# A gated recurrence and a low-rank mixer with MLP: block-diagonal state on the full array, separate q and k banks, sliced weights, a new list schedule

## The chip, the cores and the metric

The kernel runs on one core of a Trainium2 chip. The metric is the device time of one execution in microseconds (us), the median of the runs shown.

## The reference

Four batches, eight heads, 768 steps, head size 48; all inputs float32. The first half is a gated linear recurrence ("GLA") per batch and head; its outputs, joined over the heads into x of 768 x 384, go through a mixer over the sequence of rank 32 and an MLP of width 1536.

```python
for t in range(S):
    state = alpha[:, :, t, :, None] * state + einsum('bhd,bhe->bhde', k[:, :, t], v[:, :, t])
    y[:, :, t] = einsum('bhd,bhde->bhe', q[:, :, t], state)
x = y.transpose(0, 2, 1, 3).reshape(B, S, H * D)
h = x.transpose(0, 2, 1) @ U @ V
u = x + h.transpose(0, 2, 1)
out = u + maximum(u @ w_ch1, 0.0) @ w_ch2
```

## The kernel before

**Tiling.** The sequence is cut into six chunks of 128 steps. For one chunk of one batch (`stage_gla`), all eight heads stand side by side in the free dimension (8 x 48 = 384 columns), and heads go to TensorE in four pairs; a head of a pair has 64 columns or partitions for its 48, the rest is zero. Four tiles (alpha, k, q, v; 192 KB each) are loaded by SyncE's queue (line 263). ScalarE takes the logarithm of alpha (line 265, tile `lt`), TensorE forms cumulative sums over the chunk with a triangular matrix (line 272) and the chunk's totals (line 274, four matmuls of one column), ScalarE makes `ai`, `aa` and `tot` by exponentials (lines 282 to 284). GpSimd scales k and q (lines 286 and 287, tiles `rk` and `rq`) and casts v (line 267, `rv`).

TensorE transposes `rk` and `rq` by pairs (line 295) into one PSUM bank; ScalarE copies the k half, VectorE the q half into `qk` (lines 304 and 306), both after both transposes. The scores (line 321, eight matmuls with 48 rows, at rows 0 or 64 of the array) go to a pair of banks, one for the even and one for the odd heads; VectorE multiplies each with the causal mask (line 332, `pm`). The output of the chunk, y, has eight matmuls of q with the state so far (line 347, 48 rows each, at rows 0 or 64) and eight of the masked scores with v (line 352, the full array, 48 columns), in two groups of four and four for each parity. ScalarE copies y into `xb` (line 363). The state of a head pair stands at partitions 0 to 47 and 64 to 111 with 48 columns: line 376 brings the old state into PSUM with an identity of 112 rows, line 381 adds k times v (eight matmuls of 48 columns, to partitions 0 or 64), and VectorE multiplies with `tot` (line 389, `st`).

After six chunks, `stage_mix` forms U times x (line 406, four at a time in columns 0, 32, 64 and 96 of the array), multiplies with V (line 417), adds x (VectorE, line 418, `ub`), and transposes the sum (line 427, copied by ScalarE, line 435, `uT`). `mlp1` has 24 products for a batch, each of three matmuls of 384 columns (line 447), with the ReLU on ScalarE (line 455) and VectorE (line 457) in turns; `mlp2` has six of twelve matmuls (line 471); VectorE adds u (line 478, `ou`), SyncE stores (line 479).

**PSUM.** Eight banks: two pairs for scores and y (`pair`), two banks (`gen`) for everything else of GLA and mix, two (`mlp`) for the MLP. In the last batch the MLP may use all.

**What sets the order.** Each step is an entry in a plan (class `Plan`) with an engine, a cost, what it reads and writes, and a priority. `Plan.run` simulates the engines with these costs, always takes the entry that can start first (by priority among those within 1 ns), and so gets one fixed list for each engine; the engines then run their lists in order, and wait where data come later than planned. GLA has priorities of 1000 and up, the MLP 5000 and up, so GLA goes first when both are ready. Weights are loaded by GpSimd's queue, U and V at the start, w1 and w2 after y of chunks 3 and 4 of batch 0 are copied (lines 250 and 253), each in one transfer with a cast to bfloat16. The plan gives these GpSimd entries a cost, but no time on the DMA engines; loads have 960 ns each.

Of the kernel before, what the change touches and what calls it, by code (L numbers as in the profile page):

```python
# [16 lines left out]

# [5 lines left out]
class Buf:  # L23


    def __init__(self, pool=None, slot=None):
        self.pools = pool if isinstance(pool, list) else ([pool] if pool else [])
        self.slot = slot
        self.home = None
        self.idx = 0  # L30
        self.left = 0
        self.last = 0.0
# [5 lines left out]
class Op:  # L38
    __slots__ = ("eng", "cost", "fn", "prio", "deps", "bufs", "n", "end", "users", "est", "i", "keep")


class Plan:


    LAT = {"PE": 230.0, "ACT": 120.0, "DVE": 120.0, "POOL": 150.0, "SP": 0.0, "DMA": 0.0}
# [6 lines left out]
    def add(self, eng, cost, fn, r=(), w=(), prio=0.0, keep=(), after=()):  # L52
        op = Op()
        op.eng, op.cost, op.fn, op.prio = eng, cost, fn, prio
        op.i = len(self.ops)
        op.deps, op.users, op.est, op.end = set(), [], 0.0, None
        op.keep = keep
# [17 lines left out]
        for k in list(r) + list(w) + list(keep):  # L75
# [9 lines left out]
    def run(self):  # L85
# [4 lines left out]
        ready = {}  # L90
        for op in self.ops:
            if op.n == 0:
                ready.setdefault(op.eng, []).append(op)
        clock = {}
        order = []
        dma = 0.0
        todo = len(self.ops)
        while todo:
            best = None
            for eng, cand in ready.items():  # L100
                now = clock.get(eng, 0.0)
                ok = []
                for op in cand:
                    t = op.est
                    for b in op.bufs:
                        if b.slot is None:
                            s = [x for p in b.pools for x in p.free if x is not None]
                            if not s:
                                t = None
                                break  # L110
                            t = max(t, min(s))
                    if t is not None:
                        ok.append((max(t, now), op))
                if not ok:
                    continue
                t0 = min(t for t, _ in ok)
                t1, op = min(((t, o) for t, o in ok if t <= t0 + 1.0), key=lambda x: (x[1].prio, x[1].i))
                if best is None or t1 < best[0]:
                    best = (t1, eng, op)
            if best is None:  # L120
                raise RuntimeError("the plan is stuck")
            t, eng, op = best
            for b in op.bufs:
                if b.slot is None:
                    _, n, x = min((f, n, x) for n, p in enumerate(b.pools) for x, f in enumerate(p.free) if f is not None)
                    p = b.pools[n]
                    p.free[x] = None
                    b.home, b.idx, b.slot = p, x, p.slots[x]
            ready[eng].remove(op)
            if eng == "SP":  # L130
                clock[eng] = t + 450.0
                dma = max(dma, t + 450.0) + op.cost
                op.end = dma + 1800.0
            else:
                clock[eng] = t + op.cost
                op.end = t + op.cost
            order.append((t, op))
            for b in op.bufs:
                b.left -= 1
                b.last = max(b.last, op.end + self.LAT[eng])  # L140
                if b.left == 0 and b.home is not None:
                    b.home.free[b.idx] = b.last
            for u in op.users:
                u.n -= 1
                lat = 0.0 if u.eng == eng and eng == "PE" else self.LAT[eng]
                u.est = max(u.est, op.end + lat)
                if u.n == 0:
                    ready.setdefault(u.eng, []).append(u)
# [3 lines left out]
        for _, op in order:  # L152
            op.fn()


def mm(*cols):
    return sum(max(c, 54) / 2.4 + 2.5 for c in cols)
# [3 lines left out]
def kernel(  # L161
# [22 lines left out]
    W = 112  # L184
    TW = S // 2

# [9 lines left out]

    ut_ones = const.tile([C, C], BF16, name="ut_ones")
# [5 lines left out]
    ones = const.tile([C, 1], BF16, name="ones")  # L203
    nc.vector.memset(ones, 1.0)

    w1_sb = const.tile([128, NCT, F], BF16, name="w1_sb")
    w2_sb = const.tile([128, NJ, DM], BF16, name="w2_sb")
    u_sb = const.tile([128, NC, R], BF16, name="u_sb")
    vm_sb = const.tile([128, S], BF16, name="vm_sb")

    io = Pool(slots("io", 40, [C, H, D], FP32))
# [11 lines left out]
    tots = Pool(slots("tot", 4, [128, HP, 1], FP32))  # L223
    qks = Pool(slots("qk", 3, [128, 8, C], BF16))
    pms = Pool(slots("pm", 3, [C, H, C], BF16))
    sts = Pool(slots("st", 4, [128, HP, D], BF16))
# [6 lines left out]
    s_zero = const.tile([128, HP, D], BF16, name="s_zero")  # L233
    nc.gpsimd.memset(s_zero, 0.0)
# [6 lines left out]
    def bf(bank):  # L241
        return bank.bitcast(BF16)

    def load_weights():
# [286 lines left out]
```

## Time and profile before

| what | value |
|---|---|
| median of the two runs shown | 211.76 us (211.25 and 212.28) |
| span of the profiled execution | 210.8 us; the median is 0.96 us above it |
| TensorE (PE) busy | 174.7 us, 83% |
| weight loads on PE | 107.5 us |
| VectorE, ScalarE, GpSimd busy | 97.4, 91.3, 60.8 us |
| moved by DMA | 26.48 MB, mean 126 GB/s |

The profiled execution's own time is its span; what lies around it isn't recorded. PE's time is of matmuls whose ends are modelled, so that followers overlap; the distance from one start to the next is what a matmul costs in a row. PEld is the load of the stationary operand, DVE VectorE, ACT ScalarE, POOL GpSimd, SP SyncE. A row's bracket gives the idle time before it on its engine and what ended it.

### The profile page before, as it was taken

The numbers are of one execution on the slowest core, as the hardware profiler recorded it, in microseconds if no ns is written. First come the engines' busy times: TensorE is split into PE (matmuls) and PEld (weight loads), VectorE is DVE, ScalarE is ACT, GpSimd is POOL, SyncE is SP. The second block draws the span as 40 slices with busy tenths as digits, with TensorE's granted clock in tenths as the row PEclk, the third lists the DMA queues.
The fourth block names the chain that finished last, engine by engine and source line by source line (L and its number), as shares of the span: only waits on it lengthen the run. The fifth ranks groups of instructions, "written<-read, shape, count | busy, mean of one in ns | idle before, by whom it ended". The sixth has DMA issues, their size and how long they took to land.

```text
span 210.8 us, 4417 instructions
## 1 busy us (share of the span) xinstructions
PE 174.7 (83%) x1732; PEld 107.5 (51%) x1732; DVE 97.4 (46%) x196; ACT 91.3 (43%) x209; POOL 60.8 (29%) x92
## 2 busy tenths in 40 slices
PE   1367868204899999899998499999999999999993
PEld 0245646001656655465665356565465656566561
DVE  1124526002657564766646557565542544433331
ACT  3255454003586654967465744643341450320100
POOL 8544663200074454435462830420000000000000
PEclk9999999999999999999999969999999999999999
DMA  7999999999999999999999950011102001212222
GB/s 127 179 188 190 165 190 178 189 190 173 192 168 197 164 195 156 198 174 196 171 212 159 222 164 2 3 37 37 40 0 99 13 3 37 75 40 75 75 74 77
DMA packets 106244, 26.48 MB, mean 126 GB/s; under 512 B 101104, under 2 KB 105840, under 8 KB 106224
## 3 DMA queue, kind: packets, MB, share of 16 engines
q1 hardware_dynamic: 103296, 23.60, 63.5%
q0 software_dynamic: 2928, 2.61, 7.8%
q8 instruction: 13, 0.21, 0.4%
q14 instruction: 7, 0.06, 0.1%
HBM read 24.08 MB, written 4.72 MB: 137 GB/s over the span
## 4 chain that ended last, share of the span: by engine, by line
PE 57%; DMA 16%; SPq 14%; ACT 3%; issue 3%; DVE 3%; POOL 1%; POOLq 0%; ACTq 0%
PE ps L471 21%; PE ps L447 20%; SPq L263 14%; DMA io<-in_alpha_dram 11%; DMA io<-in_v_dram 4%; PE ps L295 3%; PE ps L321 3%; PE ps L352 2%; PE ps L347 2%; DMA out_dram<-ou 2%; PE ps L427 2%; PE ps L417 2%; DVE ub L418 1%; PE ps L381 1%; PE ps L272 1%
## 5 line engine op out<-in xcount | busy, mean ns | idle before, releaser
L447 PE MATMUL ps<-uT,w_sb 128*128 128x384 bf16 x288 | 54.9, 329 | 0.5 <-ACT h1t L455 0.4
L471 PE MATMUL ps<-w_sb,h1t 128*128 128x384 bf16 x288 | 51.9, 326 | 0.0
L455 ACT ACTIVATE h1t<-ps 128x384 bf16<-128x384 f32 x48 | 23.4, 491 | 38.7 <-PE ps L447 38.6
L332 DVE TENSOR_TENSOR pm<-ps,maskc 128x512 bf16<-128x512 f32 x48 | 31.5, 685 | 18.8 <-PE ps L321 18.7
L471 PEld LDWEIGHTS <-h1t 128*128 128x128 bf16 x288 | 26.8, 97 | 16.4 <-issue 0.2
L447 PEld LDWEIGHTS <-w_sb 128*128 128x128 bf16 x288 | 26.2, 98 | 16.6 <-issue 2.2
L457 DVE TENSOR_SCALAR h1t<-ps 128x384 bf16<-128x384 f32 x48 | 26.2, 555 | 16.6 <-PE ps L447 16.0
L286 POOL TENSOR_TENSOR rk<-io,ai 128x384 bf16<-128x384 f32 x24 | 21.9, 913 | 37.6 <-ACT ai L282 35.2
L478 DVE TENSOR_TENSOR ou<-ub,ps 128x384 f32<-128x384 bf16 x24 | 13.3, 553 | 30.8 <-PE ps L471 27.8
L306 DVE COPY qk<-ps 128x512 bf16<-128x512 bf16 x24 | 10.1, 422 | 35.9 <-ACT utx L414 14.6
L265 ACT ACTIVATE lt<-io 128x384 bf16<-128x384 f32 x24 | 12.6, 524 | 32.5 <-DMA io<-in_alpha_dram 32.5
L267 POOL CAST rv<-io 128x384 bf16<-128x384 f32 x24 | 12.1, 503 | 38.6 <-DMA io<-in_v_dram 35.9
L287 POOL TENSOR_TENSOR rq<-io,aa 128x384 bf16<-128x384 f32 x24 | 21.9, 911 | 0.5 <-ACT tot L284 0.3
L304 ACT COPY qk<-ps 128x512 bf16<-128x512 bf16 x24 | 14.0, 583 | 13.0 <-PE ps L295 8.6
L321 PE MATMUL ps<-qk 48*128 48x128 bf16 x192 | 11.2, 247 | 5.3 <-ACT qk L304 3.4
L363 ACT CAST xb<-ps 128x384 bf16<-128x384 f32 x24 | 11.4, 477 | 9.4 <-PE ps L352 9.1
L352 PE MATMUL ps<-rv,pm 128*128 128x48 bf16 x192 | 13.8, 193 | 1.1 <-DVE pm L332 1.0
L282 ACT ACTIVATE ai<-ps 128x384 bf16<-128x384 f32 x24 | 11.9, 494 | 6.0 <-PE ps L274 5.0
L406 PE MATMUL ps<-xb,u_sb 128*32 128x384 bf16 x24 | 3.6, 376 | 12.8 <-ACT xb L363 11.6
L295 PEld LDWEIGHTS <-rq 128*128 128x128 bf16 x96 | 7.1, 108 | 13.6 <-issue 12.4
L418 DVE TENSOR_TENSOR ub<-xb,ps 128x384 bf16<-128x384 bf16 x24 | 12.4, 550 | 3.0 <-PE ps L417 2.6
L272 PE MATMUL ps<-lt,ut_ones 128*128 128x384 bf16 x24 | 9.1, 379 | 5.3 <-ACT lt L265 5.3
(44 smaller groups left out, 164.4 us busy)
## 6 DMA issues: line engine op xcount, KB each, us to landing
io<-in_alpha_dram SPq DMA_DIRECT2D x24, 192.0 KB, 4.5
io<-in_k_dram SPq DMA_DIRECT2D x24, 192.0 KB, 4.6
io<-in_q_dram SPq DMA_DIRECT2D x24, 192.0 KB, 4.4
io<-in_v_dram SPq DMA_DIRECT2D x24, 192.0 KB, 4.5
out_dram<-ou SPq DMA_DIRECT2D x24, 192.0 KB, 1.9
w_sb<-in_moe_w_ch_dram POOLq DMA_DIRECT2D x2, 1152.0 KB, 14.1
vm_sb<-in_moe_V_dram POOLq DMA_DIRECT2D x4, 48.0 KB, 5.2
u_sb<-in_moe_U_dram POOLq DMA_DIRECT2D x1, 48.0 KB, 5.4
```

Of the source, the lines that this page charges most:

```text
L263: P.add("SP", 960, lambda t=t, src=src: nc.sync.dma_start(t(), src[b, :, sl, :].rearrange("h t d -> t h d")), w=[t], prio=kk)
L286: P.add("POOL", 930, lambda: nc.gpsimd.tensor_tensor(rk()[:, :, 0:D], kt(), ai(), op=ALU.mult), r=[kt, ai], w=[rk], prio=pr + 2)
L287: P.add("POOL", 930, lambda: nc.gpsimd.tensor_tensor(rq()[:, :, 0:D], qt(), aa(), op=ALU.mult), r=[qt, aa], w=[rq], prio=pr + 2)
L304: nc.scalar.copy(qk()[:, o : o + HP, :], t[:, o : o + HP, :])
L321: nc.tensor.matmul(s2[:, par, p, :], lhsT=qk()[o : o + D, HP + p, :], rhs=qk()[o : o + D, p, :], start=(p == 0), stop=(p == HP - 1),)
L332: nc.vector.tensor_tensor(pm().rearrange("t (hp two) c -> t two hp c", two=2)[:, par], s2[:, par], maskc.to_broadcast([C, HP, C]), op=ALU. ...
L352: nc.tensor.matmul(y2[:, p, :], lhsT=pm()[:, 2 * p + par, :], rhs=rv()[:, 2 * p + par, :], start=(p == 0 and sprev is None), stop=(p == HP ...
L418: P.add("DVE", 550, lambda c=c, hb=hb: nc.vector.tensor_tensor(ub()[:, c, :], xb()[:, c, :], hb()[:, 0:DM], op=ALU.add), r=[hb, (xb, c)], ...
L447: nc.tensor.matmul(bank(hb)[:, 0:TW], lhsT=w1_sb[:, ct, jt * 128 : (jt + 1) * 128], rhs=uT()[:, ct, tt * TW : (tt + 1) * TW], start=(ct == ...
L455: P.add("ACT", 500, lambda jt=jt, hb=hb: nc.scalar.activation(h1()[:, jt, tt * TW : (tt + 1) * TW], bank(hb)[:, 0:TW], AF.Relu), r=[hb], w ...
L457: P.add("DVE", 560, lambda jt=jt, hb=hb: nc.vector.tensor_scalar_max(h1()[:, jt, tt * TW : (tt + 1) * TW], bank(hb)[:, 0:TW], 0.0), r=[hb] ...
L471: nc.tensor.matmul(bank(hb)[:, 0:DM], lhsT=h1()[:, jt, c * C : (c + 1) * C], rhs=w2_sb[:, jt, :], start=(jt == 0), stop=(jt == NJ - 1),)
```

## The change

**GLA.** The state of a head pair becomes a block-diagonal matrix of 128 x 96. To keep the other blocks zero, the chunk's totals get a second column for each pair, with -30000 added where row and column belong to different heads (`offd`, one more matmul of 8 columns with the identity), so that their exponential is zero. The state is then brought in with a full identity (one matmul of 384 columns) and k times v added by pairs (four matmuls of 96 columns on the full array); VectorE's multiplication has 128 x 384 elements. y has four matmuls of q with the state (128 rows, 96 columns) and eight with the scores; it is one group, in one bank. The zero state at the start of a batch is no longer added.

**Banks.** All eight banks form one pool. k and q are transposed into a bank each and copied to `kT` and `qT`, each as soon as its own transposes are done. An MLP product of batches 0 to 2 takes a bank only while more than four are free (`reserve`).

**Weights.** U and V are loaded as float32 by ScalarE's queue at the start and cast by GpSimd. w1 and w2 have three tiles each, loaded by GpSimd's queue in three transfers each, w1 when v of chunk 5 of batch 0 has landed, w2 when v of the first chunk of batch 1 has; a product waits only for the slice that it reads.

**Plan.** An entry may name several engines with a cost for each, and the engine that would finish it first takes it: the copies of `kT`, `qT`, `xb`, `utx`, `uT` and the ReLUs may go to ScalarE or VectorE. Weight transfers occupy the modelled DMA engines. A change of array mode costs 95 ns in the plan; steps of batches 1 to 3 get 150 ns of slack. Loads of all batches stand first in the list, and v of a chunk follows the next chunk's alpha. The MLP's priority puts it three chunks into the next batch (`LEAD`). In batch 0 VectorE scales q.

The core of the diff, with the plan's run shortened to what it models anew:

```diff
-    def add(self, eng, cost, fn, r=(), w=(), prio=0.0, keep=(), after=()):
+    def add(self, engs, fn, r=(), w=(), prio=0.0, mode="F", slack=0.0, after=()):
...
+                        s = sorted(x for x in b.pool.free if x is not None)
+                        if len(s) <= b.reserve:
+                            t = None
+                            break
+                        t = max(t, s[b.reserve])
...
+                key = (t1, t1 + op.engs[eng])
+                if best is None or key < best[0]:
+                    best = (key, eng, op)
...
-                clock[eng] = t + 450.0
-                dma = max(dma, t + 450.0) + op.cost
-                op.end = dma + 1800.0
+                dma = max(dma, t + 600.0) + cost
+                clock[eng] = max(t + 450.0, dma - 3500.0)
+                end = dma + 1600.0
+            elif op.mode == "DMA":
+                clock[eng] = t + 1000.0
+                dma = max(dma, t + 1000.0) + cost
+                end = max(t + 1000.0 + cost, t) + 2000.0
...
-    pair = Pool([ps[:, 0:2, :], ps[:, 2:4, :]])
-    gen = Pool([ps[:, 4, :], ps[:, 5, :]])
-    mlp = Pool([ps[:, 6, :], ps[:, 7, :]])
+    bank = Pool([ps[:, i, :] for i in range(8)])
...
+    nc.scalar.dma_start(u_in, moe_U.rearrange("(c p) r -> p c r", p=128))
+    for g in range(4):
+        nc.scalar.dma_start(v_in[32 * g : 32 * g + R, :], moe_V)
...
+    def f_w1(i):
+        nc.gpsimd.dma_start(w1_sb[i], moe_w_ch1.rearrange("(c p) f -> p c f", p=128)[:, :, i * FW : (i + 1) * FW])
...
+            for t, src, o in ((at, alpha, 0.0), (kt, k, 0.1), (qt, q, 0.2), (vt, v, 1.05)):
+                load(t, src, c, kk + o)
...
+            nc.tensor.matmul(cb()[:, DM : DM + 2 * HP], lhsT=ident, rhs=offd.rearrange("p a b -> p (a b)"), start=False, stop=False)
...
+        P.add({"DVE": 420} if b == 0 else {"POOL": 885}, lambda e: f_scale(e, rq, qt, aa), r=[qt, aa], w=[rq], prio=pr + 11, slack=sl)
...
+                if sprev is not None:
+                    nc.tensor.matmul(d2, lhsT=ident, rhs=sprev().rearrange("p a d -> p (a d)"), start=True, stop=False, skip_group_check=True)
+                for p in range(HP):
+                    nc.tensor.matmul(
+                        d2[:, p * 2 * D : (p + 1) * 2 * D],
+                        lhsT=rk()[:, 2 * p : 2 * p + 2, :].rearrange("t h w -> t (h w)"),
+                        rhs=rv()[:, 2 * p : 2 * p + 2, :].rearrange("t h d -> t (h d)"),
...
+                for p in range(HP):
+                    nc.tensor.matmul(y[:, 2 * p * D : (2 * p + 2) * D], lhsT=qT()[:, p, :], rhs=sprev()[:, p, :], start=(p == 0), stop=False)
...
+    def mlp_prio(b, x):
+        return ((b + 1) * NC + LEAD + x * NC) * 100.0
...
+            hb = Buf(bank, 0 if b == B - 1 else 4)
...
+            if b == 0 and c == NC - 1:
+                vt = tiles[b, c][3]
+                for i in range(3):
+                    P.add({"POOL": 2000}, lambda e, i=i: f_w1(i), r=[vt], w=[("w1", i)], prio=c * 100.0 + 30 + i, mode="DMA")
+                vt = tiles[1, 0][3]
+                for i in range(3):
+                    P.add({"POOL": 2400}, lambda e, i=i: f_w2(i), r=[vt], w=[("w2", i)], prio=-1, mode="DMA")
```

## Rows read from the trace of the kernel before

**Rows 1.** The page's slices: busy tenths, 40 slices of 5.27 us.

```profile
PE   1367868204899999899998499999999999999993
...
PEclk9999999999999999999999969999999999999999
DMA  7999999999999999999999950011102001212222
```

**Rows 2.** Windows: length, busy us (count) of each engine, clock, DMA share, GB/s.

```profile
37.00:51.00 14.00, 1.92 (x11) 0.89 (x11) 0.00 (x0) 1.22 (x3) 1.80 (x3) 1.00 1.12 182
57.00:126.00 69.00, 63.86 (x782) 39.53 (x782) 40.95 (x82) 44.63 (x110) 33.74 (x45) 0.98 1.11 184
126.00:207.40 81.40, 80.87 (x633) 48.11 (x627) 38.49 (x74) 25.68 (x53) 3.53 (x4) 1.00 0.12 42
207.40:210.80 3.40, 0.00 (x0) 0.00 (x0) 0.55 (x1) 0.00 (x0) 0.00 (x0) 1.00 0.18 63
124.00:125.00 1.00, 1.00 (x9) 0.83 (x8) 0.45 (x1) 0.13 (x1) 0.00 (x0) 0.50 0.02 8
```

**Rows 3.** Timeline, 29 to 58 us: start, length, engine, line, idle before.

```profile
29.73 0.83 POOL L250 DMA_DIRECT2D w_sb<-in_moe_w_ch_dram  x1
...
31.68 0.49 POOL L267 CAST rv<-io 128x384 bf16<-128x384 f32 x1
...
32.12 1.09 POOL L253 DMA_DIRECT2D w_sb<-in_moe_w_ch_dram  x1
...
36.70 0.34 PE L352 MATMUL ps<-rv,pm 128*128 128x48 bf16 x4
...
49.21 0.52 ACT L265 ACTIVATE lt<-io 128x384 bf16<-128x384 f32 x1 [12.32 <-DMA io<-in_alpha_dram]
49.64 0.46 ACT L363 CAST xb<-ps 128x384 bf16<-128x384 f32 x1
...
50.15 0.48 PE L406 MATMUL ps<-xb,u_sb 128*32 128x384 bf16 x1 [11.63 <-ACT xb L363]
...
57.06 0.65 PE L447 MATMUL ps<-uT,w_sb 128*128 128x384 bf16 x3
```

**Rows 4.** DMA queues, 29 to 50 us: packets, MB, share of 16 engines.

```profile
q0 software_dynamic: 1952, 2.36, 66.4%
q1 hardware_dynamic: 7383, 1.39, 48.0%
```

**Rows 5.** The weight tile's transfers, issue to landing.

```profile
DMA to landing us min/median/max: 11.2/14.1/16.9
```

**Rows 6.** Groups by line on PE: line 272, first 0 to 57, then 57 to 126 us.

```profile
L272 PE MATMUL ps<-lt,ut_ones 128*128 128x384 bf16 x8 | 3.8, 476 | 5.3 <-ACT lt L265 5.3
...
L272 PE MATMUL ps<-lt,ut_ones 128*128 128x384 bf16 x15 | 4.9, 330 | 0.0
```

**Rows 7.** Timeline of PE, 62 to 66 us.

```profile
62.14 0.25 PE L376 MATMUL ps<-st,ident 112*112 112x192 bf16 x1
...
62.53 0.66 PE L447 MATMUL ps<-uT,w_sb 128*128 128x384 bf16 x3
63.13 0.40 PE L321 MATMUL ps<-qk 48*128 48x128 bf16 x8
63.46 0.40 PE L295 MATMUL ps<-ident,rk 128*128 128x128 bf16 x4
...
63.91 0.33 PE L272 MATMUL ps<-lt,ut_ones 128*128 128x384 bf16 x1
...
64.18 1.14 PE L447 MATMUL ps<-uT,w_sb 128*128 128x384 bf16 x6
65.25 0.27 PE L347 MATMUL ps<-st,qk 48*128 48x48 bf16 x4
...
65.85 0.27 PE L352 MATMUL ps<-rv,pm 128*128 128x48 bf16 x4
65.97 0.65 PE L447 MATMUL ps<-uT,w_sb 128*128 128x384 bf16 x3
```

**Rows 8.** The page's groups: the causal mask.

```profile
L332 DVE TENSOR_TENSOR pm<-ps,maskc 128x512 bf16<-128x512 f32 x48 | 31.5, 685 | 18.8 <-PE ps L321 18.7
```

More of the change, by code (lines that the diff above doesn't have):

```diff
@@ L38 @@
 class Op:
[L39 removed]
+    __slots__ = ("engs", "fn", "prio", "deps", "bufs", "n", "users", "est", "i", "mode", "slack", "eng", "t")
 class Plan:
[L45 removed]
+    LAT = {"PE": 215.0, "ACT": 155.0, "DVE": 145.0, "POOL": 110.0, "SP": 0.0}
+    SWITCH = 95.0
     def __init__(self):
@@ L74, in add @@
         bufs = []
-        for k in list(r) + list(w) + list(keep):
+        for k in list(r) + list(w):
             b = k[0] if isinstance(k, tuple) else k
@@ L96, in run @@
         dma = 0.0
+        mode = "F"
         todo = len(self.ops)
         while todo:
-            best = None
[L100 to L115, printed above, removed]
+            per = {}
+            for op in ready:
+                t = op.est
+                for b in op.bufs:
+                    if b.slot is None:
+                        s = sorted(x for x in b.pool.free if x is not None)
[3 more added lines that the diff above has]
+                        t = max(t, s[b.reserve])
+                if t is None:
+                    continue
+                for eng in op.engs:
+                    per.setdefault(eng, []).append((max(t, clock.get(eng, 0.0)), op))
+            best = None
+            for eng, ok in per.items():
@@ L138, in run @@
+            order.append(op)
+            done = end + (0.0 if op.mode == "DMA" else self.LAT[eng])
             for b in op.bufs:
                 b.left -= 1
-                b.last = max(b.last, op.end + self.LAT[eng])
-                if b.left == 0 and b.home is not None:
-                    b.home.free[b.idx] = b.last
+                b.last = max(b.last, done)
+                if b.left == 0:
+                    b.pool.free[b.idx] = b.last
             for u in op.users:
                 u.n -= 1
-                lat = 0.0 if u.eng == eng and eng == "PE" else self.LAT[eng]
@@ new lines, with stage_loads, load @@
+    LEAD = 3.0
+    tiles = {}
+    def stage_loads(b):
+        def load(t, src, c, key):
+            sl = slice(c * C, (c + 1) * C)
+            P.add({"SP": 1030.0}, lambda e: nc.sync.dma_start(t(), src[b, :, sl, :].rearrange("h t d -> t h d")), w=[t], prio=key)
+        for c in range(NC):
+            at, qt, kt, vt = (Buf(io) for _ in range(4))
+            tiles[b, c] = at, qt, kt, vt
+            kk = b * NC + c
+            for t, src, o in ((at, alpha, 0.0), (kt, k, 0.1), (qt, q, 0.2), (vt, v, 1.05)):
+                load(t, src, c, kk + o)
@@ L330, in f_mask @@
         def f_mask(par):
[L331 to L351 removed]
+            s2 = sc[par]().rearrange("p (hp c) -> p hp c", c=C)
@@ L352, in f_y @@
+        yb = Buf(bank)
+        def f_y(e):
+            y = yb()[:, 0:DM]
+            if sprev is not None:
+                for p in range(HP):
+                    nc.tensor.matmul(y[:, 2 * p * D : (2 * p + 2) * D], lhsT=qT()[:, p, :], rhs=sprev()[:, p, :], start=(p == 0), stop=False)
+            for h in range(H):
                 nc.tensor.matmul(
-                    y2[:, p, :], lhsT=pm()[:, 2 * p + par, :], rhs=rv()[:, 2 * p + par, :],
-                    start=(p == 0 and sprev is None), stop=(p == HP - 1),
-                )
```

336 lines of the change are left out of this document (155 added, 181 removed).

## The prediction

> **What bounds the kernel now.** I read the page's slices first [rows 1]. A digit is 5.27 us. The DMA row is full up to 121 us, while the PE row has a weak start, two nearly empty slices from 37 to 47 us (2 and 0), and is full after 58 except for a 4 from 116 to 121. So neither resource bounds the whole: loads pace the first part, TensorE the last. The stretches [rows 2] make it exact. From 37 to 51 us PE is busy 1.92 of 14 us while DMA moves 182 GB/s; from 57 to 126 it is busy 63.86 of 69; from 126 to the last matmul at 207.4 it is busy 80.87 of 81.40; the tail, an addition and the last store, takes 3.4 us. After about 57 us the end is therefore PE's remaining work plus what PE loses in it.
>
> The hole is the second thing to understand, and the timeline shows it [rows 3]. GpSimd issues both weight transfers at 29.73 and 32.12 us. The last product of batch 0 (y of chunk 5) starts at 36.70, but its copy into xb runs on ScalarE at 49.64: ahead of it in ScalarE's queue stood a logarithm that waited 12.32 us for an alpha tile. PE then waited 11.63 us for that copy, and the first MLP product came at 57.06. The queues tell why the alpha was late [rows 4]: between 29 and 50 us the weights moved 2.36 MB and the loads 1.39 MB, that is 7 tiles in 21 us where 184 GB/s would bring 19. The weights landed 11.2 and 16.9 us after issue [rows 5].
>
> The clock has to be read with care. Its row says 1.00 from the start, yet the 384-column matmul of line 272 has a mean of 476 ns before 57 us and 330 ns from 57 to 126 [rows 6]. The 146 ns between them are nearly what 384 columns differ by at 1.2 and 2.4 GHz (160 ns), so I take the early part as half clock by duration, and all terms below from the later part. Once, after the slice in which PE was at four tenths [rows 1], the granted clock itself reads 0.50, its lower level [rows 2].
>
> **The old time as a sum.** MLP products follow each other at (1.14-0.33)/5 = 0.162 us [rows 7]; 576 of them (288 on each of lines 447 and 471) are 93.6 us. A GLA chunk on PE, from one start to the next with pipelined tails taken off, costs [rows 7]: cumulative sums 63.91 to 64.18, 0.27; transposes 63.46 to 63.91, 0.45; scores 63.02 (62.53 plus three products) to 63.46, 0.44; y 65.155 (64.18 plus six products) to 65.97, 0.815; state 62.14 to 62.53, 0.39. Together 2.365 us, and 17 chunks after 57.06 are 40.2. From 57.06 to 207.40 are 150.3 us, so 16.6 remain: the mixes of batches 1 to 3 and lost time. I carry these over unchanged as one term.
>
> **The change part by part.**
> *y.* Eight 48-row state products become four full-array products of 96 columns; eight score products stay. The last four score products before an MLP product take 65.85 to 65.97, 0.03 each; the four row-tiled ones take 65.25 to 65.45, 0.05 each with the change of array mode inside. New cost: low end four of 96 columns at the MLP's rate per column (0.042) and eight at 0.03, 0.41; high end twelve at 0.05, 0.60. No mode change is left inside, so I take 0.42: 0.395 us saved.
> *State.* One 384-column product (0.162) and four of 96 columns (0.042 to 0.056, the latter being a transpose, 0.45/8) give 0.33 to 0.39 for 0.39. I take 0.36.
> *Sums.* One more product of 8 columns: 0.03, bounded by the 0.027 that each of the four one-column products takes ((0.27-0.162)/4) and 0.05.
> Transposes and scores issue as many matmuls as before. Per chunk 2.365-0.395-0.03+0.03 = 1.97 us (1.93 to 2.2).
>
> Against the first step speaks a rule. The four row-tiled products took 0.20 us [rows 7], mode change included. The Trainium skill, "TensorEngine Tiling (Array Packing)", sections Tiling Modes and Performance Considerations, gives up to 2x for a contraction of 64 rows or fewer through two row tiles at once, and says too that a change of tiling mode drains the array. The trace cannot split the 0.20 us into the two; by the first sentence alone the untiled products would give the saving back and the sum would be 201, by the second the change removes the drains and it stays at the value below.
>
> *Other engines.* The masks keep 685 ns each [rows 8]. The new state multiplication covers 192 columns more on VectorE, at the masks' rate 0.26 us; VectorE was busy 40.95 of 69 us [rows 2] and doesn't bind, so I cost it at nothing: MLP products cover the longer chain, and uncovered it is 17 x 0.26, 4.4 us. Separate banks and copies for q and k, and the scaling of q on VectorE in batch 0, shorten a chain that the loads pace there and MLP products hide later: nothing gained in the sum. The five small loads on ScalarE's queue stand ahead of the first logarithm; in the first slice PE is at one tenth [rows 1] and chunk 0 waits for loads, so a delay of some 2 us is absorbed; uncovered it would cost those 2 us.
>
> *Weights.* They wait for v of chunk 5, and w2 for v of the next batch's first chunk. The old v of chunk 5 was cast at 31.68 [rows 3]; one load is now ahead of it, so w1 goes at about 32. By the old share [rows 4] half of the bytes takes some 10 us: thirds at about 36, 39 and 42. Loads meanwhile bring one tile in about 3 us, so v of chunk (1,0) lands at about 42, and w2 runs from 42 to 52. Behind the w2 issues on GpSimd stand, by their priority of -1, the scalings and the cast of chunks (1,0) and (1,1), and PE's transposes wait for those.
>
> *Start of the MLP.* Before, 7.42 us lay between the xb copy (49.64) and the first MLP product (57.06). If the copy follows its y, at 34 to 37.5, the MLP starts at 40 to 46; I take 43, and no slice of w1 is awaited then. But chunks (1,1) and (1,2) still load at a third of the rate until 52, and a list that expects them earlier makes an in-order engine wait, as the logarithm did. I charge 2 us (0 to 8).
>
> The sum: 43 + 2 + 93.6 + 17.5 chunks x 1.97 (34.5; half of a chunk more is left at 43 than at 57) + 16.6 + tail 3.4 = 193.1 us of span. The old span of 210.8 stands 0.96 below the median of 211.76; with the same margin the forecast is 194 us, of which 12 of the gain come from the hole and 7 from y, less what the earlier start still has to do.
>
> **The rivals.**
> *Hole kept (0.12).* The slices split a transfer, not its share of the DMA engines; an alpha may again hold ScalarE for 12 us. For it: 66.4% against 48.0% for the queues in that stretch [rows 4]. Against it: w2 comes later and MLP work is there to run. With the start at 53 in place of 45 the sum gives 202.
> *Loads bind between batches 0 and 1 (0.08).* 48 tiles of 0.197 MB, the weights and the first stores are some 13 MB; at 184 GB/s the next batch's last tile lands near 72, its MLP can start near 84 (some 5 us from v's cast to y, 31.68 to 36.70, and 7.4 on), and PE's work from 45 (23.4 of MLP, six chunks of 1.97, a mix of some 2.5) ends near 83. The two meet; a few stores more and PE idles up to 5 us: 199.
> *Tiling was worth its drains (0.05).* The four full products multiply half zeros; if they take as long as the eight that ran two at a time and the mode changes were cheap, the chunk stays at 2.365: 17.5 x 0.395 = 6.9 us more, 201. The matmul part then doesn't do what it says. For it: 0.05 a product is also what untiled products could take. Against it: 0.03 a product right before an MLP product, the same array mode [rows 7]. The rule above is this case.
> *Fewer losses (0.09).* The one pool of eight banks and the new latencies remove half of some 9 us (16.6 less three mixes of 2.5) and the 2 us charged: 187 or, with a start at 41, 185.
> *Slower (0.04).* An MLP product of batches 0 to 2 takes a bank only while more than four are free; before, two banks were its own. A chunk's two score banks alone are held for one and two masks (0.685, 1.37). If waiting chunks hold four banks most of the time, MLP work slides behind the last chunk: PE loses a quarter of the 85 us from 45 to 130, 21 us, and the time is 215. It decides from about 17 us of such idling on. Against it: a chunk comes every 6.3 us (37.7/6), and its masks hold the score banks for under a quarter of that.
>
> **How the numbers follow.** My forecast case (0.62) spans 189 to 200: start 40 to 46, charge 0 to 4, chunk up to 2.05. The range of 185 to 204 adds the faster case, the first three rivals, the charge of 8 and the 2.2 us chunk. About 2% is what a measurement here can tell from no change, so faster means under 207.5. All but the slower rival and the worst of the kept hole (a second stall of the same kind after it) are under that: faster 0.91, same 0.05, slower 0.04.
>
> **What the new profile would show.** The first product of line 447's successor at 40 to 46 us; y's group at about 0.42 us between its neighbours and a chunk near 1.97; PE busy over 90% from 52 on; three w1 landings before 44, and w2 after 50. It would be wrong if PE's first dense slice is again near 57, if four 96-column products take over 0.3 us, or if PE idles between 70 and 85.

## The result and the profile after

The changed kernel takes 187.78 us (186.91 and 188.65) against 211.76: ratio 0.885, 95% interval 0.876 to 0.894. Forecast were 194, 185 to 204. On another chip, beside the experiments, it took 186.48, ratio 0.8835 (0.878 to 0.889). Times are medians of all executions shown; the ratios leave out executions more than 1.5% slower than the fastest of the same kernel. The profiled execution is the one of 188.65, with a span of 186.9; its last matmul ends at 182.9.

The page's slices, now of 4.67 us, answer to [rows 1]:

```profile
PE   0157878788999999889999969999999999999991
```

The two empty slices near 40 us are gone. What is left in their place is an emptier first slice.

Three windows, to be read against [rows 2]: the hole, the stretch from 57 to 126 us, the stretch from there to the new last matmul; and a fourth at a drop of the clock (the clock is the share of TensorE's full clock that was granted, 0.50 its lower level):

```profile
37.00:51.00 14.00, 12.82 (x113) 8.01 (x113) 8.96 (x17) 8.99 (x21) 7.07 (x10) 1.00 1.25 190
57.00:126.00 69.00, 65.82 (x754) 44.15 (x752) 44.04 (x84) 42.30 (x103) 30.21 (x41) 0.98 0.90 188
126.00:182.90 56.90, 56.64 (x452) 34.67 (x446) 20.99 (x39) 26.61 (x57) 3.53 (x4) 1.00 0.13 45
112.00:118.00 6.00, 5.70 (x54) 4.45 (x54) 2.85 (x7) 4.82 (x14) 5.49 (x7) 0.72 1.05 219
```

From 37 to 51 us PE is busy 12.82 us, where it was 1.92. From 57 to 126 us PE is a little fuller than before (65.82 of 69 us against 63.86), and there is less for it to do.

The timeline where the hole was, for [rows 3]: the load of alpha of chunk (1,1), that is chunk 1 of batch 1, the transfers of w1, the last score products of y of chunk 5, its copy into xb, the transfers of w2, the logarithm of chunk (1,1) and the first MLP product:

```profile
27.98 0.99 SPq L286 DMA_DIRECT2D io<-in_alpha_dram  x1
...
32.49 2.47 POOL L275 DMA_DIRECT2D w_sb<-in_moe_w_ch_dram  x3
...
36.56 0.46 PE L409 MATMUL ps<-rv,pm 128*128 128x48 bf16 x7 [0.38 <-DVE pm L368]
...
37.06 0.48 ACT L257 CAST xb<-ps 128x384 bf16<-128x384 f32 x1 [0.36 <-PE ps L409]
37.20 2.29 POOL L278 DMA_DIRECT2D w_sb<-in_moe_w_ch_dram  x3
...
38.48 0.53 ACT L301 ACTIVATE lt<-io 128x384 bf16<-128x384 f32 x1
...
43.99 1.14 PE L472 MATMUL ps<-uT,w_sb 128*128 128x384 bf16 x6
```

That load of alpha, from issue to landing:

```profile
DMA to landing us min/median/max: 3.7/3.7/3.7
```

The end of y of chunk 5 is no earlier than before (its last group starts at 36.56 against 36.70). But its copy now stands ahead of the logarithm in ScalarE's list and runs at 37.06 in place of 49.64, and the first MLP product comes at 43.99 in place of 57.06. A second thing changed with it: the alpha that held up ScalarE before was then issued at 30.76, behind the first weight transfer at 29.73, and landed 18.4 us later; now it is issued at 27.98, ahead of the first weight transfer at 32.49, and lands 3.7 us later. Its logarithm would not have waited even ahead of the copy. So the new order of the loads and the new list both work against this hole, and no run separates the two.

The DMA queues from 29 to 50 us, for [rows 4], and the weights from issue to landing, for [rows 5]:

```profile
q0 software_dynamic: 2525, 2.17, 65.2%
q1 hardware_dynamic: 9408, 1.78, 51.8%
```

```profile
DMA to landing us min/median/max: 6.6/10.2/13.9
```

The weights again take the larger share, but the loads got 1.78 MB where it was 1.39.

PE at 45 to 59 us, for [rows 7]:

```profile
45.85 0.65 PE L472 MATMUL ps<-uT,w_sb 128*128 128x384 bf16 x3
46.43 0.40 PE L358 MATMUL ps<-qt,kt 48*128 48x128 bf16 x8
46.76 0.40 PE L337 MATMUL ps<-ident,rk 128*128 128x128 bf16 x4
46.99 0.33 PE L308 MATMUL ps<-lt,ut_ones 128*128 128x384 bf16 x1
...
47.29 0.38 PE L337 MATMUL ps<-ident,rq 128*128 128x128 bf16 x4
47.51 1.14 PE L472 MATMUL ps<-uT,w_sb 128*128 128x384 bf16 x6
...
49.10 2.12 PE L472 MATMUL ps<-uT,w_sb 128*128 128x384 bf16 x12
51.06 0.33 PE L407 MATMUL ps<-st,qt 128*128 128x96 bf16 x4
51.23 0.36 PE L409 MATMUL ps<-rv,pm 128*128 128x48 bf16 x8
51.44 0.32 PE L381 MATMUL ps<-st,ident 128*128 128x384 bf16 x1
...
51.77 6.99 PE L472 MATMUL ps<-uT,w_sb 128*128 128x384 bf16 x42
```

Read as before: scores 46.34 (45.85 plus three products) to 46.76, 0.42; transposes 0.23 and 0.22; sums 46.99 to 47.29, 0.30; y 51.06 to 51.44, 0.38, of which the four products of 96 columns take 0.17; state to 51.77, 0.33. A chunk costs 1.88 us.

### The profile page after: what moved, and what is told of

Same layout as the page of the kernel before. It is cut to its first block, busy times and chain, and to the rows that moved or that the text cites. A ratio compares the mean times of both kernels' runs of the same rounds, so it can differ in the third digit from the quotient of the medians.

```text
span 186.9 us, 4147 instructions
## 1 busy us (share of the span) xinstructions
PE 163.1 (87%) x1592; PEld 105.7 (57%) x1592; DVE 93.5 (50%) x185; ACT 98.8 (53%) x229; POOL 57.4 (31%) x86
## 4 chain that ended last, share of the span: by engine, by line
PE 72%; DVE 5%; DMA 3%; issue 1%; ACT 1%; DVEq 0%; ACTq 0%
PE ps L472 25%; PE ps L496 25%; PE ps L337 5%; PE ps L358 3%; DMA io<-in_alpha_dram 3%; PE ps L409 3%; DVE pm L368 2%; PE ps L450 2%; DVE ub L441 2%; PE ps L308 2%; PE ps L440 2%; PE ps L383 1%; PE ps L407 1%; PE ps L381 1%; PE ps L311 1%
## 5 line engine op out<-in xcount | busy, mean ns | idle before, releaser
L472 PE MATMUL ps<-uT,w_sb 128*128 128x384 bf16 x288 | 51.9, 326 | 0.0
L483 ACT ACTIVATE h1t<-ps 128x384 bf16<-128x384 f32 x78 | 37.8, 490 | 19.3 <-PE ps L472 19.2
L326 POOL TENSOR_TENSOR rq<-io,aa 128x384 bf16<-128x384 f32 x18 | 16.5, 915 | 2.1 <-PE ps L472 2.1
L393 DVE TENSOR_TENSOR st<-ps,tot 128x384 bf16<-128x384 f32 x20 | 11.1, 554 | 8.4 <-PE ps L383 8.4
L337 PE MATMUL ps<-ident,rk 128*128 128x128 bf16 x96 | 11.1, 249 | 2.8 <-POOL rk L326 2.8
L409 PE MATMUL ps<-rv,pm 128*128 128x48 bf16 x192 | 10.6, 192 | 2.5 <-DVE pm L368 2.5
L358 PE MATMUL ps<-qt,kt 48*128 48x128 bf16 x192 | 10.8, 240 | 2.2 <-DVE qt L259 2.1
L485 DVE TENSOR_SCALAR h1t<-ps 128x384 bf16<-128x384 f32 x18 | 9.6, 556 | 6.1 <-PE ps L472 5.8
L257 ACT COPY kt<-ps 128x512 bf16<-128x512 bf16 x14 | 8.2, 588 | 7.8 <-PE ps L337 7.7
L337 PE MATMUL ps<-ident,rq 128*128 128x128 bf16 x96 | 10.8, 244 | 1.7 <-DVE rq L326 1.6
## 6 DMA issues: line engine op xcount, KB each, us to landing
w_sb<-in_moe_w_ch_dram POOLq DMA_DIRECT2D x6, 384.0 KB, 10.2
```

Source lines behind the costliest of these rows:

```text
L257: nc.scalar.copy(dst, src)
L326: eng.tensor_tensor(dst()[:, :, 0:D], a(), x(), op=ALU.mult)
L337: nc.tensor.matmul(t[:, p, :], lhsT=ring()[:, 2 * p : 2 * p + 2, :].rearrange("t h w -> t (h w)"), rhs=ident, start=True, stop=True, is_tr ...
L358: nc.tensor.matmul(sc[par]()[:, p * C : (p + 1) * C], lhsT=kT()[o : o + D, p, :], rhs=qT()[o : o + D, p, :], start=(p == 0), stop=(p == HP ...
L409: nc.tensor.matmul(y[:, h * D : (h + 1) * D], lhsT=pm()[:, h // 2, h % 2, :], rhs=rv()[:, h, :], start=(h == 0 and sprev is None), stop=(h ...
L472: nc.tensor.matmul(hb()[:, 0:TW], lhsT=w1_sb[jt * 128 // FW][:, ct, jt * 128 % FW : jt * 128 % FW + 128], rhs=uT()[:, ct, tt * TW : (tt + ...
```

## The experiments

Each kernel was timed beside the kernel before on its chip. The changed kernel was run once more beside its first three variants and is the measure for all of them; for those on other chips the ratios are the better comparison. Except in this second run and in the one with sixteen matmuls, the plan is run anew with the edit, so that a list can differ in other places too.

> The changed kernel once more, beside the others: 187 to 189 us by every theory; its interval says what differences of the others can be read.

Measured: 186.48. Its profile bears out the reading of [rows 6]. In the profiles before and after, the clock row stays at 1.00 through the whole early part; in this one it recorded early changes (windows):

```profile
30.00:40.00 10.00, 8.09 (x69) 4.55 (x68) 5.70 (x11) 4.16 (x11) 7.92 (x11) 0.50 1.13 194
...
43.00:45.00 2.00, 2.00 (x21) 1.42 (x22) 0.98 (x2) 1.20 (x3) 0.60 (x2) 1.00 1.27 184
```

The clock is half from 30 to 40 us and full from 43 on, as the durations of this kernel say too (a sum of 384 columns takes 0.48 us at 30 us in the profile after, 0.33 at 46.99).

**Old y in the new kernel.**

```diff
-        yb = Buf(bank)
+        ys = Buf(bank), Buf(bank)
...
+                    nc.tensor.matmul(y[:, p, :], lhsT=qT()[o : o + D, p, :], rhs=sprev()[o : o + D, p, par * D : (par + 1) * D], start=(p == 0), stop=False)
```

> Only y goes back to two banks, row-tiled state products of 48 rows and 48 columns in groups of four, and two copies into xb; the block-diagonal state stays. If y's matmuls carry a term of the gain, each of the 15 chunks of batches 1 to 3 that have a state costs 0.38 to 0.82 us more or less as the rows before and after show, a difference of 0.435 us, so 6.5 us more than the changed kernel: about 194. If the list and the banks carry the gain and PE had slack, 188 to 190.

Measured: 190.19, ratio 0.8998 (0.896 to 0.9036), 3.7 us more. On PE the cost is back whole:

```profile
63.95 0.81 PE L503 MATMUL ps<-w_sb,h1t 128*128 128x384 bf16 x4
64.70 0.27 PE L408 MATMUL ps<-st,qt 48*128 48x48 bf16 x4
64.90 0.27 PE L410 MATMUL ps<-rv,pm 128*128 128x48 bf16 x4
65.10 0.27 PE L408 MATMUL ps<-st,qt 48*128 48x48 bf16 x4
65.30 0.27 PE L410 MATMUL ps<-rv,pm 128*128 128x48 bf16 x4
65.42 0.38 PE L337 MATMUL ps<-ident,rq 128*128 128x128 bf16 x4
```

From 64.60 (63.95 plus four products) to 65.42 y takes 0.82 us. The three groups of four with a change of mode behind them take 0.20 us each, the last one, with none behind it, 0.12. Only the 15 chunks that have a state have the row-tiled products. So 15 times 0.435, or 6.5 us of matmul time, cost 3.7, near what the second theory said: this kernel lost less elsewhere.

The scores are row-tiled too, but their list alternates between the two halves of the rows, where y's has four of one half in a row. The products that have started by a moment tell the two apart (windows of the scores' line in the profile after, whose first product starts at 46.43, then of y's state products here, first at 64.70):

```profile
46.40:46.45 0.05, 0.02 (x2) 0.02 (x4) 1.00 0.93 134
...
64.65:64.73 0.08, 0.03 (x1) 0.04 (x2) 1.00 0.05 19
```

Of the scores two have started within 0.02 us, one of each half; of y's products one alone within 0.03.

**Sixteen matmuls without a change of mode.**

```diff
-                for p in range(HP):
-                    nc.tensor.matmul(y[:, 2 * p * D : (2 * p + 2) * D], lhsT=qT()[:, p, :], rhs=sprev()[:, p, :], start=(p == 0), stop=False)
+                for h in range(H):
+                    nc.tensor.matmul(y[:, h * D : (h + 1) * D], lhsT=qT()[:, h // 2, :], rhs=sprev()[:, h // 2, h % 2 * D : (h % 2 + 1) * D], start=(h == 0), stop=False)
```

> y's four state products of 96 columns become eight of 48 columns on the full array, the list untouched: as many matmuls as before the change, but no change of array mode. If the mode changes were the cost, eight products take 0.03 us each, 0.24 instead of 0.17, and 15 chunks add 1 us: about 189. If the number of matmuls was the cost, most of 6.5 us comes back: 192 to 194.

Measured: 187.01, ratio 0.8846 (0.88 to 0.8892): no difference from the changed kernel.

```profile
51.36 0.36 PE L407 MATMUL ps<-st,qt 128*128 128x48 bf16 x8
51.56 0.36 PE L409 MATMUL ps<-rv,pm 128*128 128x48 bf16 x8
51.76 0.32 PE L381 MATMUL ps<-st,ident 128*128 128x384 bf16 x1
```

Sixteen matmuls take 0.40 us (51.36 to 51.76), 0.025 each. The same number with two row-tiled groups among them took 0.815, or 0.41 us more for four changes of mode, some 0.1 for a change; the groups of the run before, 0.20 with a change behind and 0.12 without, say nearly the same. The number of matmuls cost next to nothing: 0.40 for sixteen against 0.38 for twelve.

**Whole weights.**

```diff
-    FW = F // 3
-    JW = NJ // 3
+    FW = F
+    JW = NJ
...
     def f_w1(i):
+        if i == 0:
```

> Each weight in one transfer at the same place of the same list. If the gates and the order close the hole and the slices do nothing, all of w1 lands near 43 to 46 us, the first MLP product moves by under 2 us from 44.0 and the time by under 2 us: 187 to 190. If the slices matter, the first MLP product waits for the whole of w1 and the time rises by 3 us or more, to 191 or above.

Measured: 186.74, ratio 0.8824 (0.8772 to 0.8875). First MLP product at 43.94. The slices do nothing here: a whole weight lands 10.3 to 13.6 us after its issue, w1 thus by about the time when uT is ready.

**The matmuls alone, in the kernel before.** The block-diagonal state, y and sums of the change; old weights, banks and plan.

```diff
+            nc.tensor.matmul(cb()[:, DM : DM + 2 * HP], lhsT=ident, rhs=offd.rearrange("p a b -> p (a b)"), start=False, stop=False)
...
+        P.add("PE", 500, f_y, r=rs + [(pm, 0), (pm, 1)], w=[yb], prio=pr)
```

> The kernel before with the block-diagonal state, its four-matmul y and state and the eight-column mask alone; weights, banks and plan stay as they were. If the matmuls are a term of their own, 17 chunks after the hole lose 0.485 us each (2.365 against 1.88 read off the traces): 8 us less, 203, with the first MLP product still near 57 us. If the saving turns into waits, because the hole and the loads set the pace, 207 to 211.

Measured: 206.49, ratio 0.9784 (0.972 to 0.9847): 4.3 us less, about half of what the matmuls save and a little under the second theory's range. First MLP product at 56.15. The clock took part of the gain: it was at its lower level here when the MLP began, from 56.15 to some 60 us, where the kernel before had three products in 0.65 us at 57.06 and so full clock (window, then the kernel's first six products):

```profile
57.00:60.00 3.00, 3.00 (x20) 1.87 (x19) 0.80 (x3) 1.74 (x4) 0.00 (x0) 0.50 1.11 219
...
56.15 2.12 PE L444 MATMUL ps<-uT,w_sb 128*128 128x384 bf16 x6
```

**The weights alone, in the kernel before.** Six slices with the later gates, their time in the plan; the loads of all batches are listed first, v still ahead of the next chunk's alpha, in 36 input tiles in place of 40.

```diff
+            elif op.keep == "DMA":
+                clock[eng] = t + 1000.0
+                dma = max(dma, t + 1000.0) + op.cost
...
+                for i in range(3):
+                    P.add("POOL", 2000, lambda i=i: f_w1(i), r=[vt], w=[("w1", i)], prio=0, keep="DMA")
```

> The kernel before with the weights alone: three slices each, w1 after v of chunk 5, w2 after v of the next batch's first chunk, time for them on the modelled DMA engines, loads first in the list; matmuls and banks stay as they were. If the hole is a term of its own, the first MLP product comes near 44 us in place of 57 and the time falls by 12 to 13 us: 198 to 199. If two MLP banks cannot use the earlier start, or loads bind between batches 0 and 1, 203 to 207.

Measured: 204.37, ratio 0.9665 (0.9579 to 0.9752), some 7 us less by the ratio. But the hole stayed (timeline):

```profile
45.59 0.52 ACT L279 ACTIVATE lt<-io 128x384 bf16<-128x384 f32 x1 [11.47 <-DMA io<-in_alpha_dram]
...
46.81 0.49 ACT L377 CAST xb<-ps 128x384 bf16<-128x384 f32 x1
...
55.47 1.12 PE L461 MATMUL ps<-uT,w_sb 128*128 128x384 bf16 x3
```

ScalarE waited 11.47 us at the logarithm of chunk (1,1), with the copy into xb of chunk 5 behind it, as before. That alpha was issued at 30.25, behind the first slice of w1 at 29.08. The gain comes from elsewhere: this kernel loses less after its start (table below). Later gates and a plan that knows of the transfers do not by themselves put the copy first, nor that alpha ahead of the weights.

**That logarithm alone, in the kernel before.**

```diff
-        P.add("ACT", 510, lambda: nc.scalar.activation(lt()[:, :, 0:D], at(), AF.Ln), r=[at], w=[lt], prio=pr + 4)
+        P.add("ACT", 510, lambda: nc.scalar.activation(lt()[:, :, 0:D], at(), AF.Ln), r=[at], w=[lt], prio=pr + 4, after=[last.get(0)] if b == 1 and c > 0 else [])
...
-                P.add("ACT", 830, f_ev, r=[ub2], w=[(uT, c // 2)], prio=pr)
+                last[b] = P.add("ACT", 830, f_ev, r=[ub2], w=[(uT, c // 2)], prio=pr)
```

> The kernel before with one rule more in its plan: the logarithms of chunks 1 to 5 of batch 1 come after batch 0's last uT copy in ScalarE's list. Matmuls, banks and weight transfers are as before. If the hole is only that logarithm waiting for an alpha tile ahead of the copy into xb, the first MLP product comes at 44 to 46 us in place of 57 and the time falls by 10 to 12 us: 199 to 201. If the transfers themselves or another engine's list keep the hole, the first product stays after 52 us and the time falls by under 5 us: 206 to 211.

Measured: 212.14, ratio 1.0121 (1.0042 to 1.0201). Both theories missed the time: the first MLP product came at 44.83, as the first one said, and nothing was gained. Window, then timeline:

```profile
52.00:66.00 14.00, 7.98 (x49) 4.38 (x49) 2.25 (x5) 5.40 (x14) 5.01 (x7) 0.51 1.20 188
```

```profile
44.83 1.14 PE L448 MATMUL ps<-uT,w_sb 128*128 128x384 bf16 x6
...
59.38 0.51 POOL L268 CAST rv<-io 128x384 bf16<-128x384 f32 x1 [3.55 <-DMA io<-in_v_dram]
...
60.82 0.36 PE L382 MATMUL ps<-rv,rk 128*48 128x48 bf16 x8 [5.29 <-POOL rk L287]
```

From 52 to 66 us PE is busy 7.98 of 14 us, at the lower clock (0.51), and one group of matmuls waits 5.29 us for a scaled k of batch 1; GpSimd, which makes it, had itself waited 3.55 us for a tile of v. The plan, which does not know of the weight transfers, had put chunks of batch 1 among the MLP products; the wait moved to other lists.

**The new plan without that knowledge.**

```diff
             elif op.mode == "DMA":
-                clock[eng] = t + 1000.0
-                dma = max(dma, t + 1000.0) + cost
-                end = max(t + 1000.0 + cost, t) + 2000.0
+                clock[eng] = end = t + 1000.0
```

> The changed kernel, except that its plan gives the weight transfers no time on the modelled DMA engines; gates and slices stay. If knowing that time is what closes the hole, an engine's list again holds something that waits for a load near 40 us, and the time rises by 3 to 12 us: 190 to 199. If the gates alone do it, 186 to 188.

Measured: 192.78, ratio 0.9147 (0.9089 to 0.9205), 6.3 us more, with the same start (timeline):

```profile
44.02 0.65 PE L470 MATMUL ps<-uT,w_sb 128*128 128x384 bf16 x3
...
52.70 0.52 ACT L299 ACTIVATE lt<-io 128x384 bf16<-128x384 f32 x1 [4.85 <-DMA io<-in_alpha_dram]
...
53.27 0.48 PE L306 MATMUL ps<-lt,ut_ones 128*128 128x384 bf16 x1 [1.87 <-ACT lt L299]
```

Again a load of batch 1 is waited for in front of MLP products, 4.85 us on ScalarE and 1.87 on PE. That is near 50 us, ten later than expected, and behind the start, not ahead of it.

**MLP shut out by banks.** Both places:

```diff
-            hb = Buf(bank, 0 if b == B - 1 else 4)
+            hb = Buf(bank, 0 if b == B - 1 else 6)
```

> The changed kernel, except that an MLP product of batches 0 to 2 takes a bank only while more than six are free, so two at most, as many as before. If the one pool of banks is what cut the lost time by some 4 us, the time rises to 189 to 191. If banks never bound, 186 to 188.

Measured: 197.62, ratio 0.9366 (0.93 to 0.9432), 11 us more, beyond both theories. A window of this kernel, then of the changed one:

```profile
60.00:80.00 20.00, 16.86 (x259) 11.98 (x259) 15.74 (x32) 15.70 (x38) 11.70 (x16) 1.00 0.98 192
```

```profile
60.00:80.00 20.00, 19.23 (x240) 12.87 (x237) 12.33 (x23) 9.98 (x26) 8.93 (x12) 1.00 0.82 182
```

PE is busy 16.86 of 20 us in place of 19.23, while VectorE, ScalarE and GpSimd are busier than there. Whether two banks are too few or the rule shuts the MLP out while GLA holds banks, the next run tells.

**Two banks of its own.** The same in `mlp2`, with `c` for `jt`.

```diff
-    bank = Pool([ps[:, i, :] for i in range(8)])
+    bank = Pool([ps[:, i, :] for i in range(6)])
+    two = Pool([ps[:, i, :] for i in (6, 7)])
...
-            hb = Buf(bank, 0 if b == B - 1 else 4)
+            hb = Buf(bank if b == B - 1 and jt % 4 else two)
```

> The changed kernel with two banks for the MLP of batches 0 to 2 alone and six for the rest, in place of the rule that more than four of eight must be free. If the number of MLP banks is what the shared pool gives, most of the 11 us of the run with more than six free comes back: 193 to 198. If what cost there was that GLA's banks shut the MLP out, own banks never do that: 186 to 189.

Measured: 185.57, ratio 0.8852 (0.8807 to 0.8897), no different from the changed kernel. Two banks are enough, so what cost in the run before was the rule with six, not the number of banks.

**q and k in one bank.** Both copies wait for both transposes, one after the other.

```diff
-        tk, tq = Buf(bank), Buf(bank)
+        tb = Buf(bank)
...
-        P.add({"DVE": 335, "ACT": 500}, lambda e: f_ev(e, kT, tk), r=[tk], w=[kT], prio=pr + 8, slack=sl)
+        x = P.add({"DVE": 335, "ACT": 500}, lambda e: f_ev(e, kT, HP), r=[(tb, "k"), (tb, "q")], w=[kT], prio=pr + 8, slack=sl)
```

> The changed kernel with q and k transposed into one bank again, each copy after both transposes, one copy after the other. If the bank each is worth nothing because MLP products cover the longer chain, 186 to 188. If the two copies one after the other let PE wait, 0.5 us for each of 15 chunks or more in part: 189 to 194.

Measured: 184.72, ratio 0.8814 (0.8749 to 0.888): a bank each is worth nothing here. This run and the one before have the lowest medians, but their intervals overlap that of the changed kernel, so neither is shown to be better.

**U and V by GpSimd's queue.** The opening of the changed kernel (timeline: ScalarE issues the loads of V, then the first logarithm):

```profile
1.28 4.97 ACTq L265 DMA_DIRECT2D v_in<-in_moe_V_dram  x4
...
6.30 0.52 ACT L301 ACTIVATE lt<-io 128x384 bf16<-128x384 f32 x1 [4.28 <-DMA io<-in_k_dram]
```

```diff
-    nc.scalar.dma_start(u_in, moe_U.rearrange("(c p) r -> p c r", p=128))
+    nc.gpsimd.dma_start(u_sb, moe_U.rearrange("(c p) r -> p c r", p=128))
```

> The changed kernel with U and V loaded by GpSimd's queue with a cast, as before, instead of by ScalarE's queue as float32. The first logarithm then starts near 3.9 in place of 6.3 us. If the later opening runs through to the first MLP product, that product comes 2 us earlier, near 42, and the time is 184 to 185. If chunk 5's loads set it anyway, 186 to 187, no change.

Measured: 190.92, ratio 0.9101 (0.9039 to 0.9162): 4.4 us slower (5.6 by the ratios), which neither theory had. The first logarithm came at 3.46 and the first MLP product at 40.04, 4 us earlier, and then (timeline and window):

```profile
40.04 1.14 PE L466 MATMUL ps<-uT,w_sb 128*128 128x384 bf16 x6
...
48.06 0.52 ACT L295 ACTIVATE lt<-io 128x384 bf16<-128x384 f32 x1 [6.35 <-DMA io<-in_alpha_dram]
...
48.63 0.48 PE L302 MATMUL ps<-lt,ut_ones 128*128 128x384 bf16 x1 [5.43 <-ACT lt L295]
```

```profile
47.00:52.00 5.00, 3.37 (x28) 2.12 (x29) 0.93 (x2) 2.76 (x8) 2.29 (x3) 0.50 0.93 185
```

With w1 issued at 28.55 and w2 at 33.26, some 4 us earlier than in the changed kernel, the alpha of chunk (1,2) is held back behind them; ScalarE waits 6.35 us for it, PE 5.43, and the granted clock reads 0.50 for 5 us.

## Why the forecast was right, and where its sum was off

The forecast's own sum, with the span of the profile after: start and charge 45.0 against 44.0, chunks 34.5 against 32.9 (17.5 of 1.88), carried term 16.6 against 12.4 (182.9 less 44.0, 93.6 and 32.9), tail 3.4 against 4.0. Together -1.0, -1.6, -4.2 and +0.6 make the 6.2 us between 193.1 and 186.9. The measured time lies in the stated range, but below the forecast case of 189 to 200; the range reached down to it for the rival of fewer losses. One product in the sum is off: 0.162 times 576 is 93.3, not 93.6. That 0.3 us only moves between two terms that are carried over together.

*Start.* Right: 43 was forecast, 43.99 measured. The forecast let the copy follow its y, and so it did; that the alpha of chunk (1,1) would be out of the way of the weights at 27.98 it did not say. The charge of 2 us was not due in this list, but its mechanism is real: it cost 5.43 us of PE's time in the run with U and V on GpSimd. That w2 would wait until 42 for v of chunk (1,0) was wrong; this v was issued at 29.02, ahead of w1, and w2 went at 37.2. The slices of w1 landed at 39.1, 42.1 and 44.6, some 3 us later than forecast, and the first MLP product did not wait for them.

*Matmuls.* y was forecast at 0.42 and took 0.38, state 0.36 and 0.33, sums 0.30 and 0.30. The rival "tiling was worth its drains" fell, and its wording was mistaken: in y's old order the two row halves were never adjacent, each group of four stood next to full-array products, and its products started one at a time; two at a time start in the scores, where the halves alternate. Of the Trainium skill, "TensorEngine Tiling (Array Packing)", section Tiling Modes, the sentence on the drain at a change of mode is the one that counted: sixteen matmuls in 0.40 us on the full array, in 0.815 with two row-tiled groups and four changes of mode among them.

What the matmuls are worth in time is less than their sum: 3.7 us in the new list for 6.5 of PE's time, 4.3 in the old for at most 8.2 (17 chunks of 0.485, fewer for those without a state). In the new list the rest is in part waits: behind the first MLP product PE idles 2.1 us in the changed kernel's second run and 0.6 with the old y. In the old list it is not: PE idles 5.3 us against 5.7, but spends 7.7 us at half clock against 3.4, which is worth some 2 us.

*The carried term* is the one that was mis-sized: 16.6 us in the sum, 12.4 in the profile after and 10.1 in the changed kernel's second one. I took lost time as a property of the stretch; the runs show that it goes with the list, and to a lesser part with the clock of the single execution. From each profile: start is the first MLP product, end the start of the last addition (us), lost is the end less start, 93.6 and the chunks (2.365 or 1.88; 17 of them for starts after 55, else 17.5; 15 times 0.435 more with the old y, 0.02 more with sixteen matmuls), with the three mixes inside. A batch's first chunk has no state and costs less than is counted, alike in every row. Idle is what PE's busy time leaves between start and end; the next column is the time there that the clock row gives as half clock:

| kernel | start | end | lost | idle | half clock | time |
|---|---|---|---|---|---|---|
| before | 57.06 | 207.40 | 16.5 | 5.7 | 3.4 | 211.76 |
| before, matmuls alone | 56.15 | 201.13 | 19.4 | 5.3 | 7.7 | 206.49 |
| before, weights and their time in the plan | 55.47 | 200.68 | 11.4 | 1.7 | none recorded | 204.37 |
| before, logarithm later | 44.83 | 206.03 | 26.2 | 12.5 | 20.5 | 212.14 |
| changed | 43.99 | 182.94 | 12.4 | 3.5 | 3.4 | 187.78 |
| changed, second run | 43.11 | 179.68 | 10.1 | 2.1 | 0 | 186.48 |
| changed, sixteen matmuls | 44.28 | 181.29 | 10.2 | 2.1 | 0 | 187.01 |
| changed, whole weights | 43.94 | 180.51 | 10.1 | 2.1 | 0 | 186.74 |
| changed, plan blind to the transfers | 44.02 | 187.96 | 17.4 | 7.8 | 3.4 | 192.78 |
| changed, six banks free | 43.86 | 191.73 | 21.4 | 9.2 | 0 | 197.62 |
| changed, own MLP banks | 43.62 | 180.04 | 9.9 | 1.6 | 0 | 185.57 |
| changed, q and k in one bank | 45.15 | 179.56 | 7.9 | 1.4 | 0 | 184.72 |
| changed, U and V on GpSimd | 40.04 | 184.24 | 17.7 | 7.5 | 6.8 | 190.92 |
| changed, old y | 43.81 | 184.52 | 7.7 | 0.6 | 0 | 190.19 |

The same kernel differs by 2.3 us of lost time between two profiles, so smaller differences say nothing. At half clock MLP products follow each other at 0.32 us in place of 0.162 (the six in 2.12 us above), so half of such a stretch counts as lost. With that and the idle time taken off, most rows keep 6.5 to 10 us, about the three mixes of some 2.5 each. With six banks free 12 are left, which is not explained; with the logarithm later it is under 4, since much of its idle time fell into stretches at half clock. The third row's profile is of that kernel's slowest execution, 205.90, and its first three products took 1.12 us, which is half clock that the row does not record.

An early start alone gave nothing: of the 26.2 us lost, 12.5 are idle, and 20.5 us ran at half clock. The plan's knowledge of the weight transfers lowers the lost time by 5 to 7 us in the new kernel, where it was taken out alone; in the old kernel it came together with gates, slices and the order of the loads, and the lost time fell by 5 there. The pool of banks (against two banks of its own), the bank each and the slices do not show in it. So the step "the hole gives 12 us" does not stand by itself: in the old list the same start gave nothing, and the new list holds it because it also fills the time behind the start. What the changed kernel's first profile lost more than its second lies in the main at 112 to 118 us, where PE waited 1.59 us for an alpha and the clock then read 0.72.

*Covers.* "A delay of some 2 us is absorbed" was wrong: the small loads kept ScalarE from its first logarithm until 6.30 where it had been 3.86, and without them the MLP started 4 us earlier. That the delay did no harm is owed to the weights, which it delayed too: luck, as the sum has it at nothing for another reason. The bank each for q and k gave nothing, as forecast. The larger state multiplication was not tried by itself.

*Rivals.* "Hole kept" did not happen to the changed kernel, but did, by the very wait named, to the old plan with the new gates. "Fewer losses" named 187, which is what came, but not for its first cause: two banks of its own did as well as the pool, so the pool is not shown to give anything. Its second cause, the new latencies, was not tried by itself. "Loads bind" did not happen: from 70 to 85 us PE is busy 13.69 of 15 us, and its waits there, of at most 0.41 us, are for masks and copies, not loads. "Slower" is a real mechanism with the wrong threshold: 11 us at more than six free banks, none at more than four.

*Open.* Which part of the new plan (costs, latencies, slack, load order) puts the copy into xb ahead of the logarithm was not tried by itself, nor was the old order of the loads in the new kernel, nor the old kernel with both the later logarithm and the weights' time. So no run shows by itself what opened the way for the start at 44 us.

## What to carry to other kernels

A fixed list is only as good as its picture of the DMA engines: a transfer that the plan left out showed up here as one engine waiting at a load with ready work behind it, and moving that one step only moved the wait. Look first at what was issued just ahead of the load that is waited for: the same alpha took 18.4 us behind a weight transfer and 3.7 ahead of it. Judge a start and the losses behind it together, since an earlier start can be lost whole. The small matmuls here paid for changes of the array mode, not for their number; count changes before counting matmuls.

## What the runs showed of the hardware

At full clock a matmul of 48 columns on the full array follows the last after 0.025 us (16 in 0.40), one of 96 after 0.043 (four in 0.17). A change between row-tiled and full-array products cost some 0.1 us (0.41 for four). Products of 48 rows in opposite halves of the array, next to each other in the list, start together (two within 0.02 us); several of the same half start one after the other. ScalarE's queue needed 4.97 us to issue four small loads at the start, and ScalarE's first instruction behind them came at 6.30, where it came at 3.46 without them. The clock row may start at 1.00 where nothing was recorded yet: the same kernel showed 0.50 from 30 to 40 us in another profile, as the durations do.
